# Threshold attention and a feed-forward block: products with v ahead of a slot's last feature tile, and a later place for one group's squares

## The chip, the cores and the metric

The kernel runs on one core of a Trainium2 chip. The metric is the device time of one launch in microseconds, of which a smaller one is better; the median over several runs is compared. A profile is one execution, taken by the hardware profiler.

The engines go by short names: PE is TensorE (its weight loads are shown as PEld), DVE is VectorE, ACT is ScalarE, POOL is GpSimd, SP is the engine whose queue issues nearly all DMAs. [...]

## The reference

Inputs are q, k and v of 8 batches x 8 heads x 576 tokens x 64, a scalar tau (0.02), a gain of 512 and two weight matrices of 512 x 2048 and 2048 x 512. All is computed in float32.

```
scores = scale * np.matmul(q, k.transpose(0, 1, 3, 2))
thresh = np.max(scores, axis=-1, keepdims=True) - tau
scores = np.where(scores >= thresh, scores, -1000000000.0)
attn = softmax(scores)                     # exp(scores - max) / sum
x = matmul(attn, v), heads side by side    # (8, 576, 512)
mu, var = mean and variance of x over its 512 features
xn = (x - mu) / np.sqrt(var + 1e-06) * g_ln
out = x + np.maximum(xn @ w_ch1, 0.0) @ w_ch2
```

## The kernel before

**Two streams on one core.** The attention is cut into 72 *slots*, nine for a batch (`SLOTS`, line 66). I call them s0 to s8. Slots s0 to s3 take the first 256 queries of each of the four head pairs, s4 the last 64 queries of all heads, s5 to s8 the second 256 queries. The feed-forward block is cut into 16 *groups* of 288 tokens, two for a batch: the even group ("first group" in the change's name, `t == 0`) and the odd one. A group's features after the first matrix are 16 *feature tiles* of 128, of four products each. The feed-forward work of a group runs in TensorE's free time in the slots that come after its tokens are ready.

**A slot** (main loop, lines 938 to 1007) issues, in this order: the scores into PSUM (`scores`, line 391; two tiles `sc` of three banks), the maxima, exponentials and the masked weights (`exponentials`, `weights`: DVE 405, ACT 416, DVE 423, with the divisions by the row sums on POOL, 436), and the turning of the weights (`turn_blocks`): DVE transposes blocks into `et` (line 501), four DMAs write `et` to a scratch buffer `scr` in DRAM (507), and in the next slot a fetch reads it back as `em` and `rest` with whole rows in place (516, 517). In batch 0 the turning is done by TensorE instead.

**The products with v** (`values_of`, line 548) of slot n are issued in slot n + 1. They write the free end of a PSUM bank of `sc[0]` (`pv_behind`, line 363), in which the scores also lie. ACT copies the result to x (565, for s4 line 556), POOL adds it to a sum over features (574). The scores of the next slot are written to that bank again and wait for the copy. `em` has one buffer.

**Where things stand in a slot.** A slot has four quarters. `at_quarter(n, i, fn)` notes a call for slot n, quarter i, and `run(n, i)` makes the calls noted: -1 behind the scores, 0 to 3 ahead of the feed-forward work of that quarter, and 4 (`QUARTERS`) behind the last. Before the change the products with v of batches 1 to 7 stand at 4: TensorE runs them as the last thing of a slot, and the next slot's scores come right behind.

**The planner** (`second_part`, lines 887 to 909). The feed-forward work of a group is a generator, `ffn_steps`, that yields once for each product (of 0.5 us on TensorE): 2 at the end of a feature tile, else 1 (the products of the second matrix, of an even group above all, yield 2 each). For each quarter the planner adds to `owed` the share of the remaining steps that falls to it: steps to the due point of the next group (`UNTIL`, `ready`) times the quarter's `ROOM`, over the sum of `ROOM` to that point. Then it takes steps while at least half a step is owed; in the first quarter and the last it goes on to the end of a tile, and `got` says where it starts from.

**The feed-forward steps** (lines 705 to 770). Behind each feature tile ACT applies the rectifier (728). At tile `d == 1` ACT squares the centred input `xc` into a buffer with the tag `sq` (739), which is there once, and POOL adds the four parts (741); at tile `var_at` (8, for odd groups 5) TensorE forms the variance from it. An odd group's last part, `winograd` (772 to 856), forms the second half of the second matrix for both groups of a batch from 14 partial sums ("fills", four products each). It holds two intermediate sums `u` in that same buffer `sq`; DVE adds them up a good while later (798, through the list `parts`), in the slots s6 and s7, in which the next batch's even group begins.

**The queue of DMAs.** SP issues in order: the fetch of `em` at the first quarter, stores, in s8, s0, s1 and s2 the loads of q and k for the slot after the next (119), stores (646), `scr` (507), in s7, s8, s0 and s1 the loads of v.

Of the kernel before, what the change touches and what calls it, by code (L numbers as in the profile page):

```python
# [18 lines left out]
def kernel(  # L19
# [39 lines left out]
    HP = H // 2  # L59
# [8 lines left out]
    NS = B * SLOTS  # L68
# [30 lines left out]
    def product(out, lhsT, rhs, **flags):  # L99


        for h in range(2):
            r = slice(64 * h, 64 * h + 64)
            nc.tensor.matmul(out[r], lhsT=lhsT[:, r], rhs=rhs, **flags)  # L104
# [570 lines left out]
    def sum_weights(i):  # L675


        out, in0, in1, op = (
            (w2_sums[:, 1], quarter(1, last_rows), quarter(1, first_rows), ALU.subtract),
            (w2_sums[:, 0], w2_sums[:, 1], quarter(0, first_rows), ALU.add),  # L680
            (w2_sums[:, 2], quarter(0, last_rows), w2_sums[:, 0], ALU.subtract),
            (quarter(1, first_rows), quarter(1, first_rows), quarter(0, first_rows), ALU.subtract),
        )[i]
        nc.gpsimd.tensor_tensor(out=out, in0=in0, in1=in1, op=op)
# [3 lines left out]
    def mean_now(g):  # L688

        if g in due:  # L690
            due.remove(g)
            mean_of(g)
            o = new_o()
            nc.scalar.copy(o, means[g])
            means[g] = o
            centre(g)
            open_o[0] -= 1
# [4 lines left out]
    def hidden_sum(out, in0, in1, op):  # L702
        nc.gpsimd.tensor_tensor(out=hidden[:, out], in0=hidden[:, in0], in1=hidden[:, in1], op=op)  # L703

    def ffn_steps(g):

        mean_now(g)
        xc = centred.pop(g)  # L710
        b, t = divmod(g, 2)
        plain = b == 0
        if g == 3:
            sum_weights(3)
        var_at = 5 if t and not plain else 8
        for d in range(ND):
            while conversion.ended < 4 * (d // 4 + 1):
                yield 0
            p1 = ps_ff.tile([128, TOK], F32, tag="ff", name="p1")
            for c in range(NK):  # L720
                product(
                    p1, lhsT=w1_sb[c][:, d * 128 : (d + 1) * 128], rhs=xc[:, c],
                    start=(c == 0), stop=(c == NK - 1),
                )
                if c < NK - 1:
                    yield 1
            at = d - 2 * HK if t and not plain and d >= 2 * HK else d
            nc.scalar.activation(hidden[:, at], p1, func=AF.Relu)  # L728
            if at < d:

                aside.append(
                    (lambda at=at, d=d: hidden_sum(at, at, d, ALU.subtract)) if at < HK
                    else (lambda at=at: hidden_sum(at - HK, at - HK, at, ALU.add))
                )
            yield 2
            if d == 1:
                run_all(parts)
                sq = ffn.tile([128, NK, TOK], F32, tag="sq", bufs=1, name="sq")
                nc.scalar.activation(sq, xc, func=AF.Square)
                for c in range(1, NK):  # L740
                    nc.gpsimd.tensor_tensor(out=sq[:, 0], in0=sq[:, 0], in1=sq[:, c], op=ALU.add)
            if d == var_at:
                var = ps_ff.tile([128, TOK], F32, tag="ff", name="var")
                product(var, lhsT=avg_sb, rhs=sq[:, 0], start=True, stop=True)
                rb = inverse[g] = ffn.tile([128, TOK], F32, tag="rb", bufs=2, name="rb")
                nc.scalar.activation(sq[:, 1], var, func=AF.Identity, bias=eps_sb)
                aside.append(lambda: root(g, rb, sq[:, 1], sq[:, 2]))
                yield 1
            if d == (2 * HK - 1 if t and not plain else ND - 1):
                rows = ND if plain else 2 * HK  # L750
                for m in range(NK):
                    p2 = ps_ff.tile([128, TOK], F32, tag="ff", name="p2")
                    for k in range(rows):
                        while conversion.ended <= conversion.n1 + 4 * m + k // 4:
                            yield 0
                        product(
                            p2, lhsT=w2_sb[:, m, k], rhs=hidden[:, k],
                            start=(k == 0), stop=(k == rows - 1),
                        )
                        if k < rows - 1:  # L760
                            yield 2
                    if plain:
                        aside.append(lambda m=m, p2=p2: into_x(g, m, p2, True))
                    else:
                        o = new_o()
                        nc.scalar.copy(o, p2)  # L766
                        parts.append(lambda m=m, o=o: into_x(g, m, o, False, True))
                    yield 2
        if t and not plain:
            yield from winograd(g - 1)  # L770
# [88 lines left out]

    QUARTERS = 4  # L860

    ROOM = (0.6, 1.0, 1.0, 0.6)
    STEPS = [
        1 + NK * ND * 2 if g < 2 else 1 + NK * ND + NK * ND // 2 + 7 * ND // 2 * (g % 2)
        for g in range(NG)
# [10 lines left out]
    def run(n, i):  # L876
        for fn, args in later_calls.pop((n, i), ()):
            fn(*args)
# [8 lines left out]
    def second_part(n, i):  # L887

        nonlocal issued, owed
        if not queue:  # L890
            return
        at = QUARTERS * n + i
        g = sum(issued >= u for u in UNTIL)
        left = sum(ROOM[t % QUARTERS] for t in range(at, ready(g + 1))) if g + 1 < NG else 0
        owed += (UNTIL[g] - issued) * ROOM[i] / left if left > 0 else 8


        got = 1 if i == 0 else 2
        while queue and (owed >= 0.5 or got == 1 and i in (0, QUARTERS - 1)):
            got = next(queue[0], None)  # L900
            if got is None:
                queue.pop(0)
                got = 1
            elif got == 0:
                owed = 0.0
                break
            else:
                issued += 1
                owed -= 1
# [28 lines left out]
    for n in range(NS):  # L938
        b, s = divmod(n, SLOTS)
        ticks = (1, 3, 4)[: 2 + n // 3] if n < 6 else range(1, 7)  # L940

        def tick(i):
            if i in ticks:
                conversion.tick()

        scores(b, s)
        if 13 <= n < 16:
            sum_weights(n - 13)
        run(n, -1)
        rest = exponentials()  # L950
        es, thr = next(rest)
        run(n, 0)
        conversion.fetch(2)
        run_all(stores)
        second_part(n, 0)
        next(rest, None)

        u = (n + 1) // SLOTS * HP + (n + 1) % SLOTS
        if (n + 1) % SLOTS < HP and u < len(units):
            turn(u)  # L960
            if u + 1 < len(units):
                load_qk(u + 1)
        run_all(aside)
        run_all(parts)
        tick(1)
        run(n, 1)
        second_part(n, 1)
        tick(2)
        blocks_go = by_blocks(b * HP)
        diags = weights(es, thr, blocks_go)  # L970
        run_all(aside)
        finish(2 if HP - 2 < s < 2 * HP else 1)
        run_all(parts)
        run_all(stores)
        tick(3)
        run(n, 2)
        second_part(n, 2)
        tick(4)
        box = []
        if blocks_go:  # L980
            scr = turn_blocks(s, es)
            at_quarter(n + 1, 0, lambda s=s, scr=scr, box=box: box.append(fetch(s, scr)))
        else:
            made = turn_weights(s, es, diags)
            at_quarter(n + 1, -1, next, made)
            at_quarter(
                n + 1, 0 if s <= HP else -1, lambda made=made, box=box: box.append(next(made))
            )
        at_quarter(
            n + 1, QUARTERS if blocks_go and n + 1 < NS else 1 if b == 0 and s <= HP else 3,  # L990
            lambda b=b, s=s, box=box: values_of(b, s, box[0]),
        )
        if s in (HP, 2 * HP):
            group_ready(2 * b + (s > HP))
        run_all(aside)
        run_all(parts)
        conversion.fetch(2)
        tick(5)
        run(n, 3)
        if b == 0 and s < HP - 2:  # L1000
            load_v(s + 2)
        elif n >= SLOTS - 2 and (n + 2) % SLOTS < HP and n < NS - 2:
            load_v((n + 2) // SLOTS * HP + (n + 2) % SLOTS)
        second_part(n, 3)
        run(n, QUARTERS)
        tick(6)
        run_all(aside)
    while later_calls or queue or aside or parts or finished or stores:
# [38 lines left out]
```

## Time and profile before

| what | us | from |
|---|---|---|
| median of 11 runs | 1488.47 (1486.69 to 1495.33) | times |
| the profiled execution | 1491.12 | its own time |
| its span | 1489.3, mean granted clock 0.985 | page |
| ACT, copy of the products (L565), x60 | 22.2 in all, 0.371 each | groups |
| POOL, sum of squares (L741), x48 | 38.7 in all, 0.805 each; 19.3 waiting for ACT sq L739 | groups |
| ACT, squares (L739), x16 | 18.7 in all, 1.168 each; 39.3 waiting for DVE o L798 | groups |
| transfer of `em`, 1024 KB, x63 | 5.3 to 8.3 from issue to landing, median 5.9 | instructions of the tile `em` |

How to read it. The span is the time from the program's first instruction to its last; the launch's own time is some 2 us more. A wait is written "engine, operation and line <- what ended it: total, times, longest". In the order of time a line has start, length, engine, line, operation, out<-in, how many, and in brackets the engine's idle time before it. The products with v go by `sc<-em,v_in`, since they are written to the free end of `sc`; both layers' products have line 104, that of a helper. A line that ends in "q" is an engine's sequencer, which issues a DMA or waits; the length of an issue is the time that the queue was held by it. A second table in that view gives, for stretches of time, the busy time of each engine and the granted clock of TensorE (PEclk, 1.00 is full).

### The profile page before, as it was taken

Reading aid. Unit: us, or ns where it says so; the run is one execution under the profiler, and the core shown is the slowest. Engines: PE = TensorE matmul, PEld = TensorE weight load, DVE = VectorE, ACT = ScalarE, POOL = GpSimd, SP = SyncE. Lnnn points to the kernel's source line nnn. Section 1 sums busy time; section 2 is a strip of 40 time slices with the busy share of each in tenths; the row PEclk is TensorE's granted clock in tenths of the full one; section 3 lists DMA queues with packets and bytes.
Section 4 is the critical chain, followed back from the end, with each engine's and each line's share of the span. In section 5 each row is a group of like instructions: output and inputs, shape, how many; then the busy total and the mean of one; then the engine's idle time right before and its main releaser. Section 6 shows DMA issues by size and latency. Waiting matters only on the chain.

```text
span 1489.3 us, 29789 instructions
## 1 busy us (share of the span) xinstructions
PE 1381.2 (93%) x11944; PEld 841.1 (56%) x11944; DVE 981.4 (66%) x1646; ACT 481.7 (32%) x978; POOL 611.2 (41%) x818
## 2 busy tenths in 40 slices
PE   5779999999999999999999899989999899998997
PEld 3656665555555555555555555555555555555554
DVE  5988856566748665787657676486656876577114
ACT  4886422132232332332323323323323223222111
POOL 2453433433355234543345433552335423453124
PEclk9999999999999999999999999999999999999999
DMA  9622476678654885377744787547854677435202
GB/s 220 175 63 74 87 169 146 159 171 181 156 148 106 171 175 151 105 166 171 166 132 105 172 174 164 151 102 165 180 137 120 158 151 180 135 96 144 48 1 33
DMA packets 466843, 205.14 MB, mean 138 GB/s; under 512 B 275024, under 2 KB 428368, under 8 KB 466704
## 3 DMA queue, kind: packets, MB, share of 16 engines
q1 hardware_dynamic: 461936, 202.64, 57.8%
q8 instruction: 94, 1.54, 0.5%
q10 hardware_dynamic: 4736, 0.59, 0.4%
q14 instruction: 45, 0.37, 0.1%
q0 software_dynamic: 32, 0.00, 0.0%
HBM read 119.41 MB, written 83.76 MB: 136 GB/s over the span
## 4 chain that ended last, share of the span: by engine, by line
PE 70%; DVE 15%; ACT 4%; DMA 4%; issue 2%; POOL 2%; SPq 2%; POOLq 0%; DVEq 0%; ACTq 0%
PE p L104 51%; PE sc L391 9%; PE sc L548 8%; DVE e L423 3%; DVE neg L405 3%; DVE o L798 2%; DVE xc L589 2%; POOL e L436 2%; DMA em<-scr 1%; DVE et L501 1%; ACT x L565 1%; PE tp L104 1%; DVE o L622 1%; DVE u L798 1%; SPq L119 1%
## 5 line engine op out<-in xcount | busy, mean ns | idle before, releaser
L104 PE MATMUL p<-xc,w 128*64 128x288 f32 x4096 | 516.0, 409 | 5.9 <-ACT hidden L728 3.8
L104 PEld LDWEIGHTS p<-xc,w 128*64 128x64 f32 x4096 | 289.8, 138 | 221.6 <-issue 14.7
L104 PE MATMUL p<-hidden,w 128*64 128x288 f32 x3200 | 398.8, 407 | 0.0
L405 DVE TENSOR_REDUCE neg<-sc 128x2 f32<-128x1152 f32 x144 | 188.7, 1352 | 287.1 <-PE sc L391 287.1
L104 PEld LDWEIGHTS p<-hidden,w 128*64 128x64 f32 x3200 | 232.7, 137 | 156.1 <-issue 5.3
L416 ACT ACTIVATE e<-sc,neg 128x576 f32<-128x576 f32 x288 | 197.4, 744 | 258.9 <-DVE neg L405 258.9
L436 POOL TENSOR_SCALAR e<-e,den 128x576 f32<-128x576 f32 x252 | 200.9, 813 | 194.9 <-DVE den L427 182.3
L423 DVE SCALAR_TENSOR_TENSOR e<-sc,thr,e 128x576 f32<-128x576 f32 x288 | 218.5, 811 | 11.1 <-ACT e L416 11.1
L391 PE MATMUL sc<-kT,qT 64*128 64x192 f32 (+3 forms) x1024 | 154.6, 437 | 57.8 <-ACT x L565 33.9
L728 ACT ACTIVATE hidden<-p 128x288 f32<-128x288 f32 x256 | 105.3, 412 | 260.0 <-PE p L104 259.3
L501 DVE STREAM_TRANSPOSE et<-e 128x1152 f32<-128x1152 f32 x112 | 151.6, 1366 | 49.5 <-POOL e L436 38.2
L391 PEld LDWEIGHTS sc<-kT,qT 64*128 64x128 f32 x1024 | 97.2, 196 | 115.0 <-ACT x L565 55.8
L409 POOL TENSOR_SCALAR thr<-neg,low_sb 128x2 f32<-128x2 f32 x144 | 43.6, 302 | 271.3 <-DVE neg L405 268.3
L548 PE MATMUL sc<-em,v_in 128*64 128x256 f32 (+1 forms) x1408 | 133.8, 334 | 12.0 <-DMA em<-scr 8.0
L623 POOL TENSOR_TENSOR x<-o,x 128x288 f32<-128x288 f32 x106 | 87.8, 828 | 125.0 <-DVE o L622 122.6
L548 PEld LDWEIGHTS sc<-em,v_in 128*64 128x64 f32 x1408 | 87.8, 139 | 53.1 <-DVE o L798 8.4
L703 POOL TENSOR_TENSOR hidden<-hidden 128x288 f32<-128x288 f32 (+1 forms) x77 | 102.0, 1334 | 16.6 <-ACT hidden L728 13.6
L104 PE MATMUL p<-hidden,w_sums 128*64 128x288 f32 x672 | 88.1, 410 | 5.7 <-ACT u L793 4.1
L574 POOL TENSOR_TENSOR sum<-sum,x 128x256 f32<-128x256 f32 (+1 forms) x64 | 32.9, 513 | 135.5 <-ACT x L565 133.0
L622 DVE TENSOR_TENSOR o<-o,rb 128x288 f32<-128x288 f32 x98 | 53.2, 543 | 42.8 <-ACT o L766 40.7
L104 PEld LDWEIGHTS p<-hidden,w_sums 128*64 128x64 f32 x672 | 46.1, 137 | 44.3 <-ACT u L793 7.2
L565 ACT COPY x<-sc 128x256 f32<-128x256 f32 x60 | 22.2, 371 | 146.1 <-PE sc L548 146.1
(153 smaller groups left out, 1003.6 us busy)
## 6 DMA issues: line engine op xcount, KB each, us to landing
scr<-et SPq DMA_DIRECT2D x252, 288.0 KB, 4.7
em<-scr SPq DMA_DIRECT2D x63, 1024.0 KB, 5.9
out_dram<-ot SPq DMA_DIRECT2D x256, 36.0 KB, 1.8
q_in<-in_q_dram SPq DMA_DIRECT2D x124, 72.0 KB, 5.8
k_in<-in_k_dram SPq DMA_DIRECT2D x120, 72.0 KB, 3.2
v_in<-in_v_dram SPq DMA_DIRECT2D x64, 128.0 KB, 4.5
rest<-scr SPq DMA_DIRECT2D x63, 128.0 KB, 5.9
w<-in_moe_w_ch_dram SPq DMA_DIRECT2D x10, 512.0 KB, 6.0
```

Of the source, the lines that this page charges most:

```text
L104: nc.tensor.matmul(out[r], lhsT=lhsT[:, r], rhs=rhs, **flags)
L391: nc.tensor.matmul(sc[h][64 * i : 64 * i + 64 if s == HP else 128, at : at + n], lhsT=ql[r] if s == HP else qT[r, half, j * 128 : (j + 1) ...
L405: nc.vector.tensor_reduce(out=neg[:, i], in_=pairs[h], axis=AXL.X, op=ALU.max, negate=True,)
L416: nc.scalar.activation(es[:, i], blocks[i], func=AF.Exp, bias=neg[:, i : i + 1])
L423: nc.vector.scalar_tensor_tensor(out=es[:, i], in0=blocks[i], scalar=thr[:, i : i + 1], in1=es[:, i], op0=ALU.is_ge, op1=ALU.mult, accum_o ...
L436: nc.gpsimd.tensor_scalar(out=es[:, i], in0=es[:, i], scalar1=den[:, i : i + 1], scalar2=1.0, op0=ALU.mult, op1=ALU.mult,)
L501: nc.vector.transpose(et[:, :, 64 * h : 64 * h + 64].rearrange("p n (j c) -> p j n c", j=2), es[:, 2 * h : 2 * h + 2].rearrange("p j (n c) ...
L548: nc.tensor.matmul(dst[64 * h : 64 * h + 64], lhsT=vt[:, c, h, :] if c < J else vr[:, h, :], rhs=pick(em[:, c] if c < J else er, hp, h), s ...
L622: nc.vector.tensor_mul(o, part, inverse[g])
L623: nc.gpsimd.tensor_tensor(out=groups[g][:, m], in0=o, in1=groups[g][:, m], op=ALU.add)
L703: nc.gpsimd.tensor_tensor(out=hidden[:, out], in0=hidden[:, in0], in1=hidden[:, in1], op=op)
L728: nc.scalar.activation(hidden[:, at], p1, func=AF.Relu)
```

## The change

The products with v of a slot are issued ahead of the last quarter's feed-forward work, not behind it. The last quarter now always takes at least one step and goes to the end of a tile, with a smaller share (`ROOM` 0.35 in place of 0.6; the third quarter has 1.25 in place of 1.0). For even groups behind batch 0 the squares, their additions and the emptying of `parts` ahead of them are issued behind feature tile 4 (the fifth) and not tile 1. The arithmetic stays the same.

```
-            if d == 1:
+
+            if d == (1 if t or plain else 4):
                 run_all(parts)
                 sq = ffn.tile([128, NK, TOK], F32, tag="sq", bufs=1, name="sq")
                 nc.scalar.activation(sq, xc, func=AF.Square)
...
-    ROOM = (0.6, 1.0, 1.0, 0.6)
+    ROOM = (0.6, 1.0, 1.25, 0.35)
...
-        got = 1 if i == 0 else 2
+        got = 1 if i in (0, QUARTERS - 1) else 2
         while queue and (owed >= 0.5 or got == 1 and i in (0, QUARTERS - 1)):
...
         at_quarter(
-            n + 1, QUARTERS if blocks_go and n + 1 < NS else 1 if b == 0 and s <= HP else 3,
+            n + 1, 1 if b == 0 and s <= HP else 3,
             lambda b=b, s=s, box=box: values_of(b, s, box[0]),
         )
...
         second_part(n, 3)
-        run(n, QUARTERS)
         tick(6)
```

More of the change, by code (lines that the diff above doesn't have):

```diff
@@ L735, in ffn_steps @@
             yield 2
-            if d == 1:
+            if d == (1 if t or plain else 4):
                 run_all(parts)
@@ L860 @@
     QUARTERS = 4
-    ROOM = (0.6, 1.0, 1.0, 0.6)
+    ROOM = (0.6, 1.0, 1.25, 0.35)
     STEPS = [
@@ L895, in second_part @@
         owed += (UNTIL[g] - issued) * ROOM[i] / left if left > 0 else 8
-        got = 1 if i == 0 else 2
+        got = 1 if i in (0, QUARTERS - 1) else 2
         while queue and (owed >= 0.5 or got == 1 and i in (0, QUARTERS - 1)):
@@ L989 @@
         at_quarter(
-            n + 1, QUARTERS if blocks_go and n + 1 < NS else 1 if b == 0 and s <= HP else 3,
+            n + 1, 1 if b == 0 and s <= HP else 3,
             lambda b=b, s=s, box=box: values_of(b, s, box[0]),
@@ L1004 @@
         second_part(n, 3)
-        run(n, QUARTERS)
         tick(6)
```

## The prediction

> **What bounds the kernel now.** I read the page first (busy time, then the chain that ended last), then TensorE's waits, then the order of time around three places, each on the engines that matter there.
>
> ```profile
> PE 1381.2 (93%) x11944; PEld 841.1 (56%) x11944; DVE 981.4 (66%) x1646; ACT 481.7 (32%) x978; POOL 611.2 (41%) x818
> PE 70%; DVE 15%; ACT 4%; DMA 4%; issue 2%; POOL 2%; SPq 2%; POOLq 0%; DVEq 0%; ACTq 0%
> PE sc L391 <- ACT x L565: 37.3, 54, 3.3
> PE sc L548 <- DMA em<-scr: 8.0, 7, 2.1
> ```
>
> The first two lines are of the page, the others of TensorE's waits (in total, times, longest). TensorE is the bound: idle for 1489.3 - 1381.2 = 108 us, a good part of it in the first 115 us. The largest of its waits is the one that the change goes for: the scores of a slot wait until ScalarE has copied the products with v out of PSUM. The second is a warning: seven times the products with v themselves waited for the transfer that brings their weights.
>
> ```profile
> 164.77 0.41 PE L104 MATMUL p<-hidden,w 128*64 128x288 f32 x2
> 165.12 2.21 PE L391 MATMUL sc<-kT,qT 64*128 64x384 f32 x16
> ```
>
> ```profile
> 728.77 1.95 PE L548 MATMUL sc<-em,v_in 128*64 128x256 f32 x16 [0.57 <-DVE sq L664]
> 730.52 0.63 PE L548 MATMUL sc<-rest,v_rest 128*64 128x256 f32 x4
> 731.61 2.21 PE L391 MATMUL sc<-kT,qT 64*128 64x384 f32 x16 [0.46 <-ACT x L565]
> ```
>
> Both are TensorE in order of time (start, length, what ran, idle time before it). At 165 scores follow a feed-forward product and start 0.06 us before its modelled end; at 731 they follow the products with v and start 0.46 us after them. From the start of the last matmul to the first score it is 0.34 us in the one, 0.88 in the other: **0.54 us a slot** is the price of the copy.
>
> ```profile
> 721.57 0.45 SPq L516 DMA_DIRECT2D em<-scr  x1
> 722.07 0.52 SPq L517 DMA_DIRECT2D rest<-scr  x1
> 722.68 4.19 SPq L119 DMA_DIRECT2D q_in<-in_q_dram  x4
> 726.91 3.33 SPq L119 DMA_DIRECT2D k_in<-in_k_dram  x4
> 730.35 1.93 SPq L646 DMA_DIRECT2D out_dram<-ot  x4
> 732.37 3.89 SPq L507 DMA_DIRECT2D scr<-et  x4
> ```
>
> This is the queue that issues the transfers. It runs without a pause from one slot's fetch of `em` to the next `scr`, 10.8 us, and in the slots that also load q and k the transposed weights (ready at 727.46) wait for it until 732.37. The fetch of 721.57 landed at 728.63, 0.14 us before the products that need it. So in these slots the products with v have no time to give away.
>
> ```profile
> 996.65 1.95 PE L548 MATMUL sc<-em,v_in 128*64 128x256 f32 x16 [1.11 <-DMA em<-scr]
> 998.40 0.63 PE L548 MATMUL sc<-rest,v_rest 128*64 128x256 f32 x4
> 1002.38 4.21 PE L391 MATMUL sc<-kT,qT 64*128 64x384 f32 x16 [3.35 <-ACT x L565]
> ```
>
> ```profile
> 1000.60 1.16 ACT L739 ACTIVATE sq<-xc 128x1152 f32<-128x1152 f32 x1 [6.54 <-DVE o L798]
> 1001.67 0.39 ACT L728 ACTIVATE hidden<-p 128x288 f32<-128x288 f32 x1
> 1001.96 0.36 ACT L565 COPY x<-sc 128x256 f32<-128x256 f32 x1
> ```
>
> TensorE and ScalarE at the end of slot s7 (I call a batch's nine slots s0 to s8). The squares of the next even group write the buffer that the Winograd sums on VectorE still read; ScalarE waits 6.54 us for them, the copy of the products queues behind, and the scores stand for 3.35 us. Then the 16 score matmuls last 4.21 us, not 2.21: the granted clock is 0.59 between 1000 and 1008 us, against 1.00 where a wait of 2.78 us went before (823 to 829).
>
> **The change, part by part.** Nothing is computed more or less; instructions change place.
>
> *1. A feature tile behind the products.* By the planner's lines, which I worked through with the old and the new ROOM, the last quarter now issues behind the products with v 3 feed-forward products in s0, s1 and s3, 4 or 5 in s2, 5 in s4 to s6, 6 in s7 and s8 (2 to 5 in batch 1), of 516.0 us / 1024 = 0.504 us each. That covers the copy (0.37 us) and its hand-over. 62 slots' products move and 61 of them have scores behind; 12 of the boundaries belong to the s6/s7 pairs of part 3. The rest: 49 x 0.54 = **-26.5 us**. If the cover were gone, the 0.54 would be back.
>
> *2. The products come earlier, the transfer does not.* What a slot's products lose is their own shift (number of products x 0.504) and twice 0.54, since two slots lie between scores and products. What they had is the distance between the fetch's landing and the end of the product before them. In us, before: s0 0.6 to 5.4; s1 -0.8 to 3.6 (7.5 once); s2 -0.6 to 3.8; s3 1.1 to 4.5; s4 5.0 to 5.7 and s5 6.3 to 6.8 (batch 1: 0.8 and -0.4); s6 8.0 to 9.8; s8 3.9 to 7.8. Shortfalls arise in s0 3.0, s1 8.9, s2 10.0, s3 5.4, s4 and s5 of batch 1 3.8, s8 1.2 us, some 32 together. A wait in one slot postpones the products of the next, whose fetch was begun from scores ahead of it, and so is taken off there: carried from slot to slot this leaves about 16 us, of which 3 are paid already: **+13 us**. Bounds: +8, if the queue's loop shortens with the slot, and +27, if no wait relieves the next. Behind these products wait ScalarE's copy and the Pool engine's sums, both of which nothing needs before the next batch half.
>
> *3. Slots s6 and s7.* From the scores of s6 to those of s8 it is 41.3 us in all six batches (2 to 7). The weights of s6 land 36.0 us after its scores (35.5 to 36.5), since VectorE transposes them late (done 22.16 us after the scores); with s6 at 19.99 - 0.54 us that is 16.5 us after the scores of s7. The end of the feed-forward products of s7 comes 14.5 us after its scores now, and 14.5 - 6 x 0.504 = 11.5 without the last six. TensorE then waits some 5 us, where it waits 1.1 to 2.2 now. The sum is 36.0 + 0.14 + 2.35 (products with v) + 6 x 0.504 - 0.04 = 41.5, plus what a slow clock costs. All waits of 2.98 to 3.35 us in this trace were followed by it; the slots behind took 22.19 and 21.02 in place of 19.33, so 1.7 to 2.9 us; I take 2.4. 43.9 - 41.3 = 2.6, times six: **+15.6 us**. In s6 the earlier products may also have to wait some 1 us until VectorE, late there, has read the scores beside them in the same bank; that comes off the wait in s7 and adds nothing.
>
> [...]
>
> *4. Squares at the fifth tile.* They move from the end of s7 into the second quarter of s8, where the Winograd sums are done. The copy no longer queues behind them; that wait lies in part 3's 41.3 already. The slow clock behind it does not: 2.86 + 1.69 us and a third like the first (scores of 4.14 us in batch 7) = **-7.4 us**. In s8 their three additions on Pool (0.805 us each) come ahead of the divisions and make the transposed weights some 1.2 us later, as in s2 now; there `scr` waits for the queue (16.1 to 17.8 us after the scores, transposes 14.5), so the cover is the queue: 0 to +1, I take **+0.5**. The product that reads them stays behind tile 8, three tiles or 12 x 0.504 = 6 us behind the new place and more than the square and the additions last (1.17 + 2.4 us).
>
> Sum: -26.5 + 13 + 15.6 - 7.4 + 0.5 = **-4.8 us**. The profiled execution took 1491.12 us (span 1489.3), 2.65 over the median of the runs; it would take 1486.3, and the median 1488.47 - 4.8 = 1483.7. Own range of this case: parts 2 and 3 at their ends, 1477 to 1491.
>
> **Rivals.**
>
> *The clock drops in many slots (slower).* Place: s1 to s3 and batch 1, where part 2 leaves waits of 1.5 to 2.1 us. Price: after the 2.16 us at 475.56 the products with v took 4.07 us and not 2.38 (as after 1.68 us at 823.71), so 1.7, and 1.3 after 2.06 us at 648.95. If the queue's loop does not shorten, about six of these waits pass 2 us: 6 x 1.5 = 9, and 4 more of waiting: 1483.7 + 13 = 1497. It decides from six waits over 2 us outside s7. Against it: 1.68 us left the clock whole.
>
> *The clock holds, and the fetches come early (faster).* If VectorE's work in s6 shifts so that the weights are transposed sooner, or the waits in s7 stay below what drops the clock: 6 x 2.4 = 14.4 us less, 1483.7 - 14.4 = 1469. For it: 2.78 us left the clock whole. Against: the wait I work out is 5.
>
> *The change doesn't do what it says (slower).* The scores may find another holder of their bank and keep the 0.54: 1483.7 + 26.5 = 1510. Against: the waits of scores for VectorE's reading (10.8 us, 8 times) all lie in the first 200 us; later the weights are done some 10 us after the scores, half a slot ahead.
>
> **How the numbers follow.** About 0.2% (3 us) is what a measurement tells from no change: below 1485.5 is faster, above 1491.4 slower. Forecast 0.46 (faster 0.25, same 0.17, slower 0.04); clock drops 0.31 (same 0.01, slower 0.30); clock holds 0.20, faster; not what it says 0.03, slower. Together 0.45, 0.18, 0.37. The time is the forecast's; the range leaves out the far half of the fast case and the far third of the slow ones: 1470 to 1497. The forecast's own is 1477 to 1491.
>
> **What would show it.** Right: the scores' wait for the copy falls from 37.3 to below 3 us; ScalarE's 39.3 us before the squares go; the products' wait for `em` grows from 8 to some 45 us, 30 of it in six waits of about 5 us in s7, each with a granted clock near 0.6 behind it. Wrong: an `em` wait below 20 us, or a clock at 1.00 behind the waits of s7 (then faster), or a scores' wait that stays. What I know least is whether VectorE's order in s6 stays as it is; each us there is 6 us in all.

## The result, and the profile after

Twelve runs of the changed kernel have a median of 1479.08 us (1475.61 to 1483.6), against 1490.47 us over 47 runs of the kernel before that were timed on the same chips: the ratio is **0.9925 [0.9915, 0.9936]**, some 11 us faster where 4.8 were forecast. The profiled execution took 1475.61 us with a span of 1473.8, which is the fastest of its kernel's runs; against the profile of before it is 15.5 us shorter, so some 4 us of what follows are the difference between two single executions.

First the page (busy time and the chain that ended last), then the first two and a later line of TensorE's waits (in total, times, longest):

```profile
PE 1379.6 (94%) x11944; PEld 845.9 (57%) x11944; DVE 982.9 (67%) x1646; ACT 482.6 (33%) x978; POOL 610.7 (41%) x818
PE 73%; DVE 13%; DMA 5%; POOL 2%; issue 2%; ACT 2%; SPq 1%; POOLq 0%; DVEq 0%; ACTq 0%
```

```profile
PE sc L548 <- DMA em<-scr: 22.8, 7, 5.5
PE sc L391 <- DVE e L423: 11.0, 9, 7.2
...
PE sc L548 <- DVE e L423: 4.3, 6, 0.7
```

ScalarE's 4% of the chain have become 2%, and the DMAs' 4% are 5%. The scores' wait for the copy (37.3 us) is gone from the list. The products with v are now what waits: 22.8 us by name for the fetch, more under other names that ended in the same moment. Measured slot by slot as TensorE's idle time ahead of these products, it is 28.0 us in the six slots s7 of batches 2 to 7 and 8.0 in all slots but these and s6. The third line is the bank in s6 that VectorE still reads.

An undisturbed slot's end, TensorE in order of time (start, length, operation, how many):

```profile
726.32 0.61 PE L548 MATMUL sc<-rest,v_rest 128*64 128x256 f32 x4
726.75 2.11 PE L104 MATMUL p<-xc,w 128*64 128x288 f32 x16
728.79 2.21 PE L391 MATMUL sc<-kT,qT 64*128 64x384 f32 x16
```

Products with v, one feature tile, scores, with no idle time between them. Slot s5, with 28 products in both kernels, is 18.20 us long and was 18.81.

A slot s7, in the same view, and then the granted clock around this wait and another one (stretch, its length, busy time of the five engine rows, PEclk, share of the DMA engines, GB/s):

```profile
983.25 3.08 PE L104 MATMUL p<-xc,w 128*64 128x288 f32 x24
990.39 3.51 PE L548 MATMUL sc<-em,v_in 128*64 128x256 f32 x16 [4.06 <-DMA em<-scr]
993.71 0.61 PE L548 MATMUL sc<-rest,v_rest 128*64 128x256 f32 x4
994.14 3.09 PE L104 MATMUL p<-xc,w 128*64 128x288 f32 x24
997.16 2.21 PE L391 MATMUL sc<-kT,qT 64*128 64x384 f32 x16
```

```profile
988.00:996.00 8.00, 5.61 (x36) 3.75 (x38) 6.55 (x9) 0.78 (x2) 5.96 (x7) 0.79 0.59 143
645.00:653.00 8.00, 5.66 (x30) 3.65 (x32) 5.15 (x7) 0.37 (x1) 4.67 (x6) 0.57 0.70 168
```

TensorE stands 4.06 us until the fetch lands, and the first 16 products then take 3.51 us in place of 1.90 to 1.95. The scores at 997.16 start at once and take 2.21 us; before, they stood 3.35 us behind the squares here and then took 4.21. The squares themselves are in the next slot, between two rectifiers of ScalarE, with no wait:

```profile
1003.67 0.44 ACT L728 ACTIVATE hidden<-p 128x288 f32<-128x288 f32 x1
1003.96 1.20 ACT L740 ACTIVATE sq<-xc 128x1152 f32<-128x1152 f32 x1
1005.39 0.41 ACT L728 ACTIVATE hidden<-p 128x288 f32<-128x288 f32 x1 [0.23 <-PE p L104]
```

The queue of DMAs behind a slot s7:

```profile
657.73 0.45 SPq L516 DMA_DIRECT2D em<-scr  x1
658.23 0.51 SPq L517 DMA_DIRECT2D rest<-scr  x1
662.00 1.96 SPq L119 DMA_DIRECT2D q_in<-in_q_dram  x4
664.00 2.13 SPq L119 DMA_DIRECT2D k_in<-in_k_dram  x4
666.23 1.94 SPq L646 DMA_DIRECT2D out_dram<-ot  x4
669.93 3.76 SPq L507 DMA_DIRECT2D scr<-et  x4
```

It now has pauses: 3.3 us ahead of the loads of q, and 1.8 ahead of `scr`, which goes out when its data are ready. The long s7 gives the queue time to catch up. This is what the forecast missed, as the experiments show.

**Where the time went.** Sums over batches 2 to 7, from the start of a slot's scores to that of another's, in us (s8 to s2 is the five stretches between these batches), for the kernels that the text below uses:

| kernel | s3 to s5 | s6, s7 | s8 to s2 | ratio to before |
|---|---|---|---|---|
| before | 335.6 | 247.9 | 387.4 | |
| the change | 326.2 | 261.6 | 371.4 | 0.9925 [0.9915, 0.9936] |
| squares alone | 335.6 | 237.0 | 385.6 | 0.9885 [0.9857, 0.9914] |
| products alone | 326.8 | 260.9 | 373.7 | 0.992 [0.9892, 0.9947] |
| change, s7's products at the end | 326.6 | 234.4 | 393.6 | 0.988 [0.9856, 0.9904] |
| that without loads of k | 325.4 | 238.0 | 375.6 | 0.9757 [0.9734, 0.978] |
| change, wait of s7 filled | 326.4 | 249.2 | 377.1 | 0.9896 [0.9869, 0.9924] |
| before, products in another bank | 326.0 | 234.1 | 383.8 | 0.9805 [0.9781, 0.983] |
| change, old shares | 326.7 | 263.8 | 378.5 | 1.0001 [0.9983, 1.0019] |

### The profile page after: what moved, and what is told of

Read it like the earlier page. It is cut to its first block, busy times and chain, and to the rows that moved or that the text cites. A ratio compares the mean times of both kernels' runs of the same rounds, so it can differ in the third digit from the quotient of the medians.

```text
span 1473.8 us, 29780 instructions
## 1 busy us (share of the span) xinstructions
PE 1379.6 (94%) x11944; PEld 845.9 (57%) x11944; DVE 982.9 (67%) x1646; ACT 482.6 (33%) x978; POOL 610.7 (41%) x818
## 4 chain that ended last, share of the span: by engine, by line
PE 73%; DVE 13%; DMA 5%; POOL 2%; issue 2%; ACT 2%; SPq 1%; POOLq 0%; DVEq 0%; ACTq 0%
PE p L104 52%; PE sc L548 10%; PE sc L391 9%; DVE e L423 3%; DMA em<-scr 3%; DVE neg L405 2%; DVE xc L589 2%; DMA scr<-et 2%; DVE o L799 2%; POOL e L436 2%; PE tp L104 1%; DVE o L622 1%; SPq L507 1%; ACT e L416 1%; DVE u L799 1%
## 5 line engine op out<-in xcount | busy, mean ns | idle before, releaser
L104 PEld LDWEIGHTS p<-xc,w 128*64 128x64 f32 x4096 | 295.2, 138 | 213.6 <-issue 14.1
L548 PE MATMUL sc<-em,v_in 128*64 128x256 f32 (+1 forms) x1408 | 140.9, 346 | 40.3 <-DMA em<-scr 22.8
L391 PE MATMUL sc<-kT,qT 64*128 64x384 f32 (+3 forms) x1024 | 150.5, 425 | 20.0 <-DVE qT L351 10.0
L391 PEld LDWEIGHTS sc<-kT,qT 64*128 64x128 f32 x1024 | 94.2, 191 | 77.5 <-issue 23.5
```

Of the source, the lines that this page charges most:

```text
L391: nc.tensor.matmul(sc[h][64 * i : 64 * i + 64 if s == HP else 128, at : at + n], lhsT=ql[r] if s == HP else qT[r, half, j * 128 : (j + 1) ...
L548: nc.tensor.matmul(dst[64 * h : 64 * h + 64], lhsT=vt[:, c, h, :] if c < J else vr[:, h, :], rhs=pick(em[:, c] if c < J else er, hp, h), s ...
```

## The experiments

**1. The squares alone**, in the kernel before.

```
-            if d == 1:
+            if d == (1 if t or plain else 4):
```

> The kernel before with the squares alone moved. My theory: before, the squares set the 41.3 us from the scores of s6 to those of s8; without them the fetch for the products with v does: 36.0 + 0.14 + 2.35 + 0.5 = 39.0 us, so 6 x 2.3 = 14 us less, and the slow clock behind the waits of about 3 us goes (7.4 us). Some 3 us come back as waits for fetches in s0 to s2. Together 18 us less than before, ratio 0.988, more than the whole change brings. Rival: the squares' wait only hid another one, and the gain is the clock's alone: 7 us, ratio 0.995. Second rival: the boundaries bring all, the squares nothing: 1.000.

Ratio 0.9885 [0.9857, 0.9914]: the theory's 0.988, and more than the whole change brings, though the two intervals all but touch (0.9914 and 0.9915). TensorE at the end of an s7 there:

```profile
822.53 1.95 PE L548 MATMUL sc<-em,v_in 128*64 128x256 f32 x16 [1.48 <-DMA em<-scr]
824.28 0.63 PE L548 MATMUL sc<-rest,v_rest 128*64 128x256 f32 x4
825.38 2.21 PE L391 MATMUL sc<-kT,qT 64*128 64x384 f32 x16 [0.47 <-ACT x L565]
```

The scores wait 0.47 us for the copy where the squares held them for 2.78 in this slot before. In this batch s6 and s7 are 38.8 us together; 39.0 were worked out from the landing of the fetch. In the mean of all six they are 39.5, since the clock dropped in two of them behind waits of 2.2 and 2.4 us.

**2. The products alone**, that is the changed kernel with its squares put back.

```
-            if d == (1 if t or plain else 4):
+            if d == 1:
```

> The changed kernel with the squares back behind the second tile. My theory: the products' copy now stands ahead of the squares on ScalarE, and TensorE waits so long for the fetch in s7 that VectorE has left the buffer by the time the squares come; so it differs from the whole change by 0 to 3 us, ratio to before 0.9925 to 0.995. Rival: the squares still hold ScalarE, and with it the rectifier and the exponentials of s8, by the 6.5 us of before: 6 x 2 to 3 us more, ratio 1.000 or above.

Ratio 0.992 [0.9892, 0.9947], as the whole change. ScalarE has no idle time at all ahead of the squares (39.3 us before), though they stand in s7 as before: TensorE waits so long for the fetch that VectorE is done. So the two parts do not add: each frees s7 of the squares, and the products' part then lengthens it. Set upon the squares alone, moving the products costs some 6 us (0.9885 to 0.9925).

**3. The products of s6 at the end of s7 again**, the rest as changed.

```
-            n + 1, 1 if b == 0 and s <= HP else 3,
+            n + 1, 1 if b == 0 and s <= HP else QUARTERS if blocks_go and s == HP + 2 else 3,
...
         second_part(n, 3)
+        run(n, QUARTERS)
```

> The changed kernel, but the products with v of s6 alone stand behind the last quarter of s7 again. My theory: s7 is set by the landing of the fetch; with no feed-forward products behind, from the scores of s6 to those of s8 it is 39.0 us where it is 43.6 with the whole change, and the waits of 4 to 5.7 us in s7 shrink to some 2 us, too short for the slow clock: 6 x 4.6 = 27 us less, of which 5 come back as waits for fetches in s0 to s2, whose queue has less time to catch up; ratio to before 0.978. Rival: the queue of DMAs sets the length of a batch, and what s7 loses comes back in s0 to s3: ratio 0.99 as with the change.

Ratio 0.988 [0.9856, 0.9904], the rival's rather than mine. s6 and s7 lose the 27 us that were expected (261.6 to 234.4), and s8 to s2 take 22 of them back (371.4 to 393.6). Its queue of DMAs in s8:

```profile
487.15 0.45 SPq L516 DMA_DIRECT2D em<-scr  x1
487.64 0.51 SPq L517 DMA_DIRECT2D rest<-scr  x1
488.26 3.93 SPq L119 DMA_DIRECT2D q_in<-in_q_dram  x4
492.23 3.08 SPq L119 DMA_DIRECT2D k_in<-in_k_dram  x4
495.41 3.45 SPq L646 DMA_DIRECT2D out_dram<-ot  x4
498.97 3.89 SPq L507 DMA_DIRECT2D scr<-et  x4
...
507.42 0.45 SPq L516 DMA_DIRECT2D em<-scr  x1
```

No pause from one fetch to the next (the rows left out are four loads of v, to 507.23): 20.27 us, longer than TensorE's work in such a slot (18.76 us with the change). TensorE's idle time ahead of the products with v, outside s6 and s7, is 26.0 us here and 8.0 with the change.

**4. The products with v in another bank**, in the kernel before.

```
-        if b == 0 and s <= HP:
+        if b == 0 and s <= HP or by_blocks(b * HP):
             pv = ps_ff.tile([128, QH], F32, tag="ff", name="pv")
```

> The kernel before, but the products with v go to one of the feed-forward block's two PSUM banks, so that no scores wait for the copy; nothing changes place, the squares neither. My theory: 0.54 us a boundary, 49 times, 26 us less, and in s6 and s7 38.5 in place of 41.3 us and no slow clock, 6 x 2.8 + 7 = 24 less; some 8 come back as waits for fetches, since every slot is shorter. Ratio 0.972. Rival: with one bank fewer the feed-forward tiles wait for the copy in place of the scores, 0.3 to 0.5 us a slot: ratio 0.99 to 1.00. Second rival: the scores wait for something else that lasts as long: 1.000.

Ratio 0.9805 [0.9781, 0.983]: short of the 0.972 expected, but by its ratio the fastest kernel of this study save one that leaves loads out (median 1463.98 us). The boundary:

```profile
757.23 0.60 PE L548 MATMUL pv<-rest,v_rest 128*64 128x256 f32 x4
757.76 2.21 PE L391 MATMUL sc<-kT,qT 64*128 64x384 f32 x16
```

Scores directly behind the products, with nothing between. The sums say the rest: s3 to s5 gain what the change gains there (326.0), s6 and s7 fall to 234.1, and only s8 to s2 stay long (383.8). The copy and the bank were what the scores waited for.

**5. The wait of s7 filled with work**, in the changed kernel.

```
+        if b > 1 and s == HP + 2:
+            warm = ps_ff.tile([128, TOK], F32, tag="ff", name="warm")
+            for i in range(8):
+                product(warm, lhsT=avg_sb, rhs=w1_sb[0][:, :TOK], start=True, stop=True)
```

> The changed kernel with eight more products, whose result nobody reads, on TensorE ahead of the products with v in s7 of batches 2 to 7: 8 x 0.5 = 4 us of work inside the wait of 4.2 to 5.6 us. My theory: the wait becomes too short for the slow clock, the granted clock behind it stays at 1.00, and though TensorE does more, s7 becomes 1.3 to 2.7 us shorter (2.0 in the mean): 12 us less than with the change, of which the queue of DMAs takes a part back; ratio to before 0.985 to 0.988. Rival: the slow matmuls come from something else than the wait (contention with the transfer that has just landed): time as with the change, 0.9925, or above by the added work.

Ratio 0.9896 [0.9869, 0.9924], between the two. TensorE in an s7, and the granted clock around it (0.79 and 0.57 above):

```profile
809.95 4.05 PE L104 MATMUL warm<-w,avg_sb 128*64 128x288 f32 x32
815.41 1.95 PE L552 MATMUL sc<-em,v_in 128*64 128x256 f32 x16 [1.41 <-DMA em<-scr]
```

```profile
800.00:830.00 30.00, 28.59 (x234) 17.28 (x233) 24.72 (x45) 9.94 (x19) 12.65 (x18) 1.00 0.65 162
```

The clock is 1.00 here, and also around two others of the six slots (975 to 1000 and 1150 to 1170 us); in the mean of the profiled execution it is 0.993, where it is 0.984 with the change. The same 16 products take 1.95 us, and s6 with s7 is 12.4 us shorter in all (261.6 to 249.2): 2.1 us a slot, with 4 us more work in each. So it was the wait that slowed them, not the transfer that had just landed. Of the 12.4 us, s8 to s2 take 5.7 back.

**6 and 7. The loads of k on ScalarE's queue**, in the kernel of experiment 3 and in that of experiment 8:

```
-                load_qk(u + 1)
+                load_qk(u + 1, (nc.sync, nc.scalar))
```

> The kernel with the products of s6 at the end of s7, whose gain did not come through, and in it the loads of k issued by ScalarE's queue, four issues of 0.5 to 1 us fewer on SP's in s8, s0, s1 and s2. Theory: SP's queue sets the length of these slots (it ran from one fetch to the next without a pause, 20.3 us); some 3 us fewer a slot undo the 24 us that s8 to s2 took back there, and the ratio to before falls from 0.988 to 0.975. Rival: the transfers themselves, not their issue, fill the time; then the ratio stays at 0.988. Second rival: ScalarE is held by the issues, the rectifier late, and the ratio rises above 0.99.

> The last kernel with the loads of k on ScalarE's queue. If the issue on SP's queue binds s8 to s2, the waits for fetches there go and the ratio falls by 0.007 or more against the last; if the transfers bind, it stays; if ScalarE is held, it rises.

Ratios 1.0319 [1.0283, 1.0354] and 1.003 [1.0013, 1.0047], where the same kernels without this edit have 0.988 and 0.9826. ScalarE is held, as the second rival had it, but less than a new wait costs that none had. ScalarE in an s8 of the first of the two, and lines of SP's waits in that kernel:

```profile
869.89 0.32 ACTq L119 DMA_DIRECT2D k_in<-in_k_dram  x1
870.12 0.76 ACT L416 ACTIVATE e<-sc,neg 128x576 f32<-128x576 f32 x1
870.25 2.44 ACTq L119 DMA_DIRECT2D k_in<-in_k_dram  x3
872.74 0.41 ACT L728 ACTIVATE hidden<-p 128x288 f32<-128x288 f32 x1 [1.86 <-PE p L104]
```

```profile
SPq L137 <- DMA k_in<-in_k_dram: 80.6, 15, 7.2
...
SPq L133 <- DMA k_in<-in_k_dram: 32.9, 10, 6.3
```

The issues hold the engine to 872.69 and the rectifier comes behind them, for which TensorE waits 0.78 us. But SP now waits ahead of its loads of v (lines 133 and 137) until loads of k have landed, 113 us in 25 places (94 us in 28 places in the second kernel), and the next fetch stands behind these loads. No data pass from k to v. The semaphores in the two traces show where the wait comes from: behind 200 us all DMAs take turns at eight of them, and each of these 25 and 28 waits is for the very semaphore that the waiting load of v will raise when it lands, and that a load of k, issued late on ScalarE's queue, had not yet raised. That is how this program shares its semaphores; a limit of the queues is not shown by it. So this pair does not tell how much of the queue's time is issue.

**8. Other bank and squares together** (experiments 4 and 1 in one kernel).

> The kernel before with the products with v in a feed-forward bank and the squares moved, nothing else. Theory: with the other bank the squares no longer stand between the products and the scores (the copy waits, the scores don't), so moving them adds only what the exponentials of s8 lose behind them: 0 to 5 us, ratio 0.977 to 0.9805. Rival: the gains add, 17 us more: 0.969.

Ratio 0.9826 [0.9798, 0.9854], a little above the theory's range, whose end (0.9805) the interval holds: with the other bank, the squares no longer stand between products and scores, and moving them is worth nothing that can be told.

**9 and 10. No loads of k from the third batch on**, in the kernel of experiment 3 and in the changed kernel (`kept` holds the tile of the last k that was loaded):

```
+            if name == "k" and u >= 2 * HP:
+                tiles.append(kept[0])
+                continue
```

> The kernel with the products of s6 at the end of s7, and no loads of k from the third batch on: every unit there uses the k of the second batch's last head pair, so the output is not the reference's. Four issues (3.2 us) and 288 KB fewer on SP's queue in s8, s0, s1 and s2, nothing put on another engine. Theory: the queue took back the gain of that kernel, so most of the 24 us in s8 to s2 comes out: ratio to before 0.974 to 0.978, against 0.988 with the loads. Rival: something else than the queue (VectorE's and ScalarE's work per slot) sets s8 to s2: 0.986 to 0.988.

> The changed kernel with no loads of k from the third batch on, as in the run beside it (the output is not the reference's). Theory: with the whole change the waits of s7 give the queue its time, and all waits for fetches outside s6 and s7 are 7 us above those of before; so at most those come out, 3 to 8 us: ratio 0.987 to 0.9905. Rival: if the queue binds here too, 15 us or more: 0.983.

Ratios 0.9757 [0.9734, 0.978] and 0.9863 [0.9846, 0.988]. In the first, s8 to s2 fall from 393.6 to 375.6 us, and the whole kernel is 18 us shorter (0.988 to 0.9757). In the changed kernel the same loads are worth some 9 us (0.9925 to 0.9863), a little over the 3 to 8 expected, and in s8 to s2 only 2.3 (371.4 to 369.1). That is the queue as the second bound: with s7 short it sets the next four slots, with s7 long it has caught up. It shows the queue and its transfers together; which of the two is open.

**11. Another order on SP's queue**, in the kernel of experiment 8. The first `run_all(stores)` stands ahead of the writes of `scr`, the last one behind them:

```
-        run_all(stores)
+        if not blocks_go:
+            run_all(stores)
...
-        elif n >= SLOTS - 2 and (n + 2) % SLOTS < HP and n < NS - 2:
-            load_v((n + 2) // SLOTS * HP + (n + 2) % SLOTS)
+        elif s >= SLOTS - 2 and n < NS - 2:
+            load_v((b + 1) * HP + s + 2 - SLOTS)
+        elif b and s in (HP - 2, HP - 1):
+            load_v(b * HP + s)
+        if blocks_go:
+            run_all(stores)
```

> The kernel with the products in a feed-forward bank at the end of the slot and the squares moved, and in it another order on SP's queue: the stores behind the slot's writes of scr, where the queue waits for these to land, and v of the third and fourth head pair in s2 and s3 in place of s0 and s1. Theory: the queue's loop from fetch to fetch falls from some 20 to 17 or 18 us, and the waits of 1.8 to 2.9 us for fetches in s0 and the slow clock behind some of them go: 10 us, ratio 0.975 to 0.977 against 0.9826. Rival: the loop is made of the transfers, and their order changes nothing: 0.9826.

Ratio 0.9999 [0.9981, 1.0017]: 26 us lost, and neither theory had it. The queue in an s6:

```profile
633.28 3.80 SPq L507 DMA_DIRECT2D scr<-et  x4
637.13 6.08 SPq L646 DMA_DIRECT2D out_dram<-ot  x8
643.32 0.39 SPq L516 DMA_DIRECT2D em<-scr  x1
```

In s6 there are eight stores, not four; behind `scr` they put off the fetch that s7 waits for, to 6.2 us behind the writes where it is 4.0 without them, and all six waits of s7 (3.5 to 4.8 us) were followed by the slow clock (0.979 in the mean of the profiled execution, 0.990 in that of experiment 8). s6 and s7 go from 231.9 to 256.2 us, while s8 to s2 stay (387.1 and 386.9).

**12. The old shares of the quarters.**

```
-    ROOM = (0.6, 1.0, 1.25, 0.35)
+    ROOM = (0.6, 1.0, 1.0, 0.6)
```

> The changed kernel with the old shares of the quarters (0.6, 1.0, 1.0, 0.6): by the planner's lines the last quarter then issues 5 to 7 products behind the products with v in s0 to s6 and s8 where the change has 3 to 6, and 6 in s7 as before. Theory: a tile of cover hides the copy already, and what is issued behind it beyond that only takes time from the fetch: about 1 us more shift in s0 to s3, where no time is left, some 8 us of waits in all, s7 as it was: ratio to before 0.997 to 0.9995. Rival: the shares matter little, since a wait in one slot is relieved in the next: 0.9925.

Ratio 1.0001 [0.9983, 1.0019]: the whole gain goes, 11 us where 8 were expected. s3 to s5, where the fetch has time to spare, stay at 326.7; s8 to s2 rise by 7.1 us and s6 and s7 by 2.2. One feature tile of cover is enough for the copy, and each product more behind the products with v is time taken from the fetch.

## Why the prediction was right, and where its sizes were off

It forecast a small gain made of large terms of both signs, and that is what the two profiles show, term by term. No errors cancelled to make it come out: part 2 was 7.3 us too dear and part 3 1.9, and -4.8 less these is -14.0, against -15.5 between the two profiles.

*Part 1, the boundaries: -26.5 us.* Right. s3 to s5, which nothing else touches, fall from 335.6 to 326.2, 0.52 us a slot; slots with the same products in both kernels gain 0.57 (s8 of batch 4, 19.33 to 18.76) to 0.61. Experiments 4 and 2 show the mechanism.

*Part 2, fetches that come too late: +13 us.* Right in kind, wrong in size, and with it the sum: outside s6 and s7 these waits grew by 5.7 us (2.3 to 8.0), less than even the lower bound. With the 28.0 us of s7 the products wait 36.0 us, where 45 were named as the sign. The step that failed is the queue's loop "from one slot's fetch of `em` to the next `scr`", which I carried from slot to slot as the trace of before had it, down to a lower bound of +8. In the longer s7 of the changed kernel the queue catches up: in s8 and s0 `scr` starts 15.0 to 16.6 and 16.5 to 18.0 us after the scores, where it was 16.2 to 17.8 and 16.6 to 18.7 (s0 of batches 3 to 7). With s7 short and all else as in the change (experiment 3) these waits are 26.0 us, 23.7 more than before and near the upper bound of +27. Experiments 5, 9 and 10 show the exchange too: what s7 loses, s8 to s2 take back.

*Part 3, s6 and s7: +15.6 us.* They grew by 13.7. The waits are the five microseconds worked out (4.06 to 5.48, six times), and all six were followed by the slow clock, 0.50 in each. Its price was 2.4 in the sum; by the slots (their length, less the time to the fetch's landing and 0.13 us from there to the products, 2.38 for the products with v and 6 x 0.504) it was 1.3 to 2.7 with a mean of 2.0 us, and experiment 5 has 2.1. The spread is that of the time at 0.50: 3.41 us behind the waits of 4.06, 4.25 and 4.78 us, for a price of 1.3 to 1.5, and 6.83 us behind those of 4.43, 5.00 and 5.48, for one of 2.2 to 2.7.

By these traces it is not the length of a wait alone that decides. Slow matmuls also came behind shorter ones, of 2.2 and 2.4 us in experiment 1 and of 2.06 and 2.16 in the kernel before, while one of 2.78 there left the clock whole. Three stretches of the kernel before, the first two soon after the waits of 2.16 and 2.06 us, the third from the end of the one of 2.78 (stretch, its length, busy time of the five engine rows, PEclk, DMA):

```profile
475.81:479.22 3.41, 3.41 (x19) 2.39 (x16) 3.00 (x4) 0.77 (x1) 1.36 (x3) 0.50 0.28 50
649.89:653.30 3.41, 2.72 (x14) 1.38 (x10) 2.47 (x4) 1.30 (x2) 1.36 (x3) 0.50 0.30 62
828.87:835.00 6.13, 6.13 (x50) 3.81 (x52) 3.38 (x4) 1.67 (x3) 3.77 (x7) 1.00 0.76 179
```

*Part 4, the squares: -7.4 + 0.5 us.* Right for the change: slots of 22.19 and 21.02 us have become 18.76, and the transposed weights of s8 come 0.4 us later (14.9 us after the scores). The cover is no longer the queue: in three of five slots `scr` goes out right behind them, at 15.0 us, still earlier than before. But it was sized inside the change only. That the squares alone would be worth 17 us, more than all parts together, stood in the numbers (41.3 against a fetch that allowed 39.0) and was not drawn from them.

*The rivals.* The clock did not drop in s0 to s3 (a wait of 2.03 us there left it whole), the waits of s7 were not short enough to spare it, and the scores found no other holder of their bank.

## What to carry to other kernels

A wait at the end of a stage can be removed by moving work into it or by taking away what is shared; where a transfer lands just in time, the second is better, since the first takes from the transfer what it gives to the engine (0.9925 against 0.9805 here). Before moving an instruction earlier, write down how much earlier its latest input lands than it is used, in every stage, and only then the price of the wait. Where a wait may slow the clock, as here, that price belongs in the sum: all six waits of 4.06 to 5.48 us paid it, 2.0 us in the mean, while of three of 2.06 to 2.78 us in the kernel before the longest did not. A queue that runs without a pause in some stages is a second bound: time saved in the stage ahead of them comes back there, and more instructions in it hurt where the count of them is highest.

## What had not been expected of the hardware

Work without a use can pay: 4 us of products inside each 5 us wait raised the granted clock from 0.984 to 0.993 in the mean and made the slot 2.1 us shorter. Loads of k that were put on ScalarE's queue to relieve SP's made SP wait for their landing, 113 us in all, and the kernel 4.4% slower (0.988 to 1.0319); the cause is in the program, whose DMAs share eight semaphores. And whether a wait of 2 to 3 us slows the clock is not settled by its length: in the kernel before, waits of 2.06 and 2.16 us were followed by a clock of 0.50, and one of 2.78 us by 1.00.
